# A fused bucketed attention and expert layer: row products split into gate products and plain transposes, with the head and tail order rewritten

## The chip, the core and the metric

The kernel runs on one core of a Trainium2 chip. Times are device microseconds (us) of one execution. The profile is one further execution of the same program, with every instruction of every engine recorded. Engines are called as in the profile: PE (TensorE matmul), PEld (its weight load, which runs beside PE), DVE (VectorE), ACT (ScalarE), POOL (GpSimd), SP (the engine that issues most transfers).

## The reference

```python
def attention(q, k, v, proj):                    # 4 batches, 8 heads, 768 rows, 64 columns
    mask = bucket(q @ proj > 0) == bucket(k @ proj > 0)     # 6 bits each
    scores = where(mask, q @ k.T / 8, -1e9)
    return softmax(scores) @ v

def experts(x, w_gate, w1, w2):                  # x: 3072 rows of 512
    logits = x @ w_gate                          # 8 experts
    e = argmax(logits); gate = softmax(logits)[e]
    return gate * (relu(x @ w1[e]) @ w2[e])      # 512 -> 1024 -> 512
```

## The kernel before

**Attention.** The 32 heads are taken as 16 pairs of heads (`g`), each pair as two halves of 384 query rows (`u`, 32 in all). A pair has 12 score units (`S0` to `S11`, one tile of 128 queries against 768 keys each, four products in fp32r). DVE takes the maximum (`R`), ACT the exponential (`X`), PE transposes the result in blocks of 128 (`T`), ACT or DVE copies them out (`E`), PE multiplies with V (`V`, 24 instructions for one half), ACT copies the result to the tile `ot` (`O`), which has the 128 columns of the two heads as partitions and 384 rows.

**Back to rows.** The step `K` (`tok`) turns `ot` into rows: for each of three blocks of 128 rows one f32 product with `ot` as the loaded weights and the 144 columns of `wgt` as the moving side. The 144 columns are 8 gate columns of the one head, an identity of 128, and 8 gate columns of the other head, so that one product gives rows and logit parts. `L` (`tok_ev`, DVE) scales them by 1/sum into `xr`. An f32 product is two MATMUL instructions, each with a weight load of its own; a plain transpose is one.

**Experts.** `route` (steps `r`) finds each row's expert and its slot, `scatter` (steps `c`) has POOL write three blocks of rows to `sorted_rows` in DRAM. Phase 0 are the first 256 rows of the largest expert, phase 1 the rest of its 512 rows; `rows(1)` loads these after the last scatter. `mm1` (steps `m`) and `mm2` are the two products; `xt` transposes the next phase's rows. Within `mm2(0, 1, mid)` the function `mid` calls `xts(1, (0, 1))`, the first two of the four transposing steps of phase 1. Weights are split into two fp32r parts by POOL (steps `v`, 1.9 us each).

**What sets the order.** Every engine works its instructions in program order. The order of the attention is written out by hand in three lists of step names: `HEAD` for pair 0, `PLAN` for pairs 1 to 14, `LAST` for pair 15, where a trailing `-` means the pair before. A letter at the end of a step (`A`, `V`, `P`, `a`, `v`) says which engine takes it. In `HEAD` the steps `k q j l p` cut the inputs into fp32r parts, `y` are the bucket products, `b` their signs, `f0` and `f1` the two parts of score unit 0, `i2` two idle products. Before `HEAD`, `warmth` issues `WARM` idle products on PE.

Of the kernel before, what the change touches and what calls it, by code (L numbers as in the profile page):

```python
# [7 lines left out]
F32 = mybir.dt.float32  # L8
# [7 lines left out]
B, H, S, D = 4, 8, 768, 64  # L16
# [25 lines left out]
FILL = 512  # L42
NONE = 1 << 20
TMAX = 24
WARM = 8


def tiles_of(n):
# [5 lines left out]
def lsh_attention_moe(ctx, tc, qk, qk2, v, proj, wg, w1, w2, out):  # L54
# [97 lines left out]
    def late_consts():  # L152
        tri = const.tile([128, 128], BF16, name="tri")
        nc.vector.tensor_scalar(tri, jp, 0.0, None, op0=OP.is_gt)
        C.update(tri=tri, ones=ones)
        C["desc"] = iota_f([128, E], [[-1, E]], "desc", base=E)
        C["base0"] = iota_f([128, E], [[ROW, E]], "base0")
        C["base"] = const.tile([128, E], F32, name="base")
        nc.vector.tensor_copy(C["base"], C["base0"])
        C["tokid"] = iota([128, B * NT], [[128, B * NT]], "tokid", cm=1)  # L160
        C["spacer"] = const.tile([1, 1], F32, name="spacer")
        nc.gpsimd.tensor_copy(wgt[:, :, E:PW - E], ident[:, None, :].to_broadcast([128, NP, 128]))
        empty_rows()

        C["oh"] = const.tile([128, 2 * 3 + 1, E], BF16, name="oh")
        nc.vector.memset(C["oh"], 0.0)
        C["ohs"] = const.tile([128, 2, 4, E], BF16, name="ohs")
        nc.vector.memset(C["ohs"], 0.0)
        C["ex"] = const.tile([128, 2 * 3, E + 1], F32, name="ex")
        nc.vector.memset(C["ex"], 1e-9)  # L170
# [198 lines left out]
    def tok(u):  # L369

        p = ps.tile([128, 512], F32, name="t", bufs=2)
        ot = OT.pop(u)
        x = p[:, :3 * PW].rearrange("p (t w) -> p t w", t=3)
        for t in range(3):
            nc.tensor.matmul(x[:, t], ot[:, t * 128:(t + 1) * 128], wgt[:, u // 2 % NP], start=True, stop=True)  # L375
        return x

    def tok_ev(u, p):
# [362 lines left out]
    def yout(n, j, mid=None):  # L741
        r, o, c = PH[n]
        if j >= len(tiles_of(c)):
            return
        i, pw = tiles_of(c)[j]
        if n + 1 == len(PH) and j + 1 == len(tiles_of(c)):
            youts(n, j, i, pw)
            return
        p = ps.tile([128, 512], F32, name="s", bufs=3)
        if by_token(n):  # L750
            k = 0
            for f in range(8):
                w = CH[4 * r + 2 + f // 4]
                for a, b in ((0, 0), (1, 0), (0, 1)):
                    nc.tensor.matmul(p[:pw], HH[n][b][:, f, i:i + pw], w[:, a, f % 4],  # L755
                                     start=(k == 0), stop=(k == 23))
                    k += 1
                    if k == 12 and mid:
                        mid()
        else:  # L760

            yw = max(pw, min(128, CAPS[1] - i))
            for m in range(4):
                nc.tensor.transpose(p[:yw, m * 128:(m + 1) * 128], YT[n][:, m, i:i + yw], ident)  # L764
        y = (P2["p"] if n else moe).tile([128, DM], F32, name="y" if n else "ye", bufs=3 if n else 2)
        nc.vector.tensor_scalar(y[:pw], p[:pw], GT[n][:pw, j:j + 1], None, op0=OP.mult)  # L766
        nc.gpsimd.memset(C["spacer"], 0.0)
        st = nc.gpsimd.indirect_dma_start(out=out, out_offset=bass.IndirectOffsetOnAxis(ap=IX[n][:pw, j:j + 1], axis=0),  # L768
                                          in_=y[:pw], in_offset=None, bounds_check=N - 1, oob_is_err=False)
        for q in outs:  # L770
            tc.declare_no_dep(st.ins, q.ins, reason="rows of other tokens")
        outs.append(st)
# [29 lines left out]
    load_x(2)  # L802
    load_x(3)
    load_v(0)
    for s in range(2):
        nc.sync.dma_start(wgt[:, :, s * (PW - E):s * (PW - E) + E], wg[:, :, s * E:(s + 1) * E])
    NC = NU // 2
    routes, parts, pick = {}, list(range(16)), pick_first()

    def weights(n):  # L810
# [8 lines left out]
    SPLITS = ((0, 0), (0, 1), (0, 2), (0, 3), (1, 0), (1, 1), (1, 2), (1, 3), (0, 4), (0, 5), (1, 4), (1, 5))  # L819

    HEAD = """
        k01V y01 k00A j01V j00P p00A y00 i2 q00V l00V b03 p01P b02 b00 q01P f0 b01 q10P k11A f1 p10A j11P y11 R0
        k10A S1 q11A j10P b13 G R1 X0 l10P y10 S2 b10 b12 s01 S3 X1 p11P R2 l01P H S4 b11 X2 R3 T00 E00a T01 w S5
        E01a R4 X3 T02 s00 E02a R5 T10 l11P X4 s10 S6 X5 E10v T11 S7 R6 E11a T12 s13 E12a R7 T20 X6 S8 s12 T21 E20v
        X7 S9 s03 s11 E21v T22 R8 s14 T30 E22a s02 S10 E30a R9 T31 z0 V0 E31a s15 X8 X9 M0 z1 s04 T32 O0 R10 S11 s05
        E32a T40 X10 R11 K0
    """.split()

    PLAN = """
# [4 lines left out]
    """.split()  # L834

    LAST = """
        S0 E40a- L0- X11- T41- R0 T42- E41a- S1 E42a- T50- R1 S2 T51- X0 E50a- X1 S3 R2 E51a- T52- S4 E52v- R3 T00
        T01 X2 E00a S5 E01a R4 T02 X3 V1- X4 E02v R5 X5 x0 M0 O1- M1- T10 T11 g0 E10v S6 E11a h0 T20 T12 R6 E20a S7
        E12a K1- R7 T21 S8 L1- X6 X7 S9 E21v T22 R8 E22a T30 x2 V0 R9 X8 E30a X9 g2 h2 T31 O0 S10 E31a T32 R10 T40
        E32a S11 K0 X10 v1 m0 R11 L0 E40a T41 m1 v1 r0 X11 E41a T42 v1 m2 u0 E42a d0 u1 d1 T50 r0 m3 T51 u2 r0 d2 v1  # L840
        E50a M1 v1 u3 T52 E52v E51a d3 m4 v1 u4 V1 d4 v1 v1 r0 O1 r0 K1 r0 r0 m5 L1 r1 u5 c0 r1 m6 r1 d5 u6 r1 m7 r1
        r1 r1 d6 c1 u7 d7
    """.split()

    DEAL = {"R5": 1, "E12a": 2, "T20": 1, "R8": 1, "M0": 1}
# [49 lines left out]
    def step(g, w):  # L895
# [29 lines left out]
        elif op == "K":  # L925
            TK[2 * n + int(x)] = tok(2 * n + int(x))
        elif op == "L":
            tok_ev(2 * n + int(x), TK.pop(2 * n + int(x)))
        elif op == "G" and n + 1 < NG:
            lsh_mm(n + 1)  # L930
        elif op == "H" and n + 1 < NG:
            lsh_ev(n + 1)
            if n:
                lsh_bits(n + 1)
        elif op in "kjqlp":
            cut(op, int(x[0]), int(x[1]), x[2])
        elif op == "y":
            lsh_first(int(x[0]), int(x[1]))
        elif op == "b":
            bits_first(int(x[0]), int(x[1]))  # L940
        elif op == "f":
            if x == "0":
                before(0)
            score(0, (x == "1",))
        elif op == "i":
            warmth(ps.tile([128, 2, 512], F32, name="s", bufs=3)[:, 0], int(x))
        elif op == "s":
            split(2 + int(x[0]), int(x[1]))
        elif op == "z":
            mask(2 + int(x))  # L950
        elif op == "w":
            lsh_bits(1)
        elif op in "xgh":
            xt_first(op, int(x))
        elif op == "m":
            mm1(0, int(x))
        elif op in "ud":
            relu(op, int(x))
        elif op == "r":
            go(last[int(x)], 1)  # L960
# [141 lines left out]
```

## Time and profile before

| | |
|---|---|
| Median of three runs | 774.7 us (771.43, 774.7, 774.88) |
| The profiled execution's own time | 777.09 us |
| its span, first to last instruction | 775.3 us |
| PE busy, share of the span | 763.9 us, 99% |
| PEld, ACT, POOL, DVE busy | 81%, 62%, 61%, 55% |

The span is what the instructions take; 1.8 us of the profiled execution lie around it. A busy PE is not PE at its peak, since the ends of its pipelined instructions are modelled; the pace is better read from one start to the next.

### The profile page before, as it was taken

The page shows a single profiled execution, that of the slowest core. Times are in us where ns is not written, and L with a number is a line of the kernel's source. Part 1 is how long each engine was busy: PE and PEld are TensorE (multiplying, and loading weights), DVE is VectorE, ACT ScalarE, POOL GpSimd, SP SyncE. Part 2 cuts the span into 40 slices and gives each one's busy share as a digit, 9 for nine tenths or more (in the row PEclk, how much of TensorE's full clock was granted, in tenths as well). Part 3 has the DMA queues.
Part 4 walks back from the last instruction along what each step waited for, and adds up shares of the span by engine and source line. Part 5 has one row for each costly group of instructions (what it writes and reads, how often), then busy time and mean ns, then how long its engine had stood idle before and what let it go on. Part 6 is the DMA issues. An engine that isn't in the chain of part 4 may idle for free.

```text
span 775.3 us, 13575 instructions
## 1 busy us (share of the span) xinstructions
PE 763.9 (99%) x4819; PEld 631.0 (81%) x4819; DVE 426.6 (55%) x1017; ACT 478.3 (62%) x936; POOL 474.8 (61%) x584
## 2 busy tenths in 40 slices
PE   9999999999999999999999998999999999999996
PEld 4777878777787777778778786989999999989895
DVE  6766766867676776667688653222454522232221
ACT  5888878878887887888788731443434444434320
POOL 7675465578635767754777482784665656668532
PEclk9999999999999999999999999999999999999998
DMA  7488844245314344530533225663445466545200
GB/s 268 163 254 271 296 160 154 70 149 185 128 62 163 123 137 160 163 103 21 163 128 120 82 95 169 233 225 105 167 140 178 144 111 197 169 149 185 101 10 36
DMA packets 48229, 115.12 MB, mean 148 GB/s; under 512 B 8851, under 2 KB 12691, under 8 KB 48160
## 3 DMA queue, kind: packets, MB, share of 16 engines
q1 hardware_dynamic: 41328, 97.88, 38.7%
q0 software_dynamic: 6688, 16.35, 6.2%
q8 instruction: 38, 0.62, 0.3%
q14 instruction: 31, 0.25, 0.1%
q10 hardware_dynamic: 144, 0.02, 0.0%
HBM read 88.39 MB, written 26.33 MB: 148 GB/s over the span
## 4 chain that ended last, share of the span: by engine, by line
PE 90%; issue 4%; POOL 2%; DVE 1%; DMA 1%; ACT 1%; SPq 0%; POOLq 0%; another core or an unknown queue 0%; DVEq 0%; ACTq 0%
PE t L320 17%; PE s L698 16%; PE t L356 16%; PE s L735 10%; PE s L288 9%; PE s L286 9%; PE s L755 6%; PE t L375 3%; PE t L244 2%; PE t L660 2%; PE s L764 1%; POOL w L626 1%; POOL sorted_rows L449 1%; PE t L222 1%; DVE m L296 1%
## 5 line engine op out<-in xcount | busy, mean ns | idle before, releaser
L296 DVE TENSOR_REDUCE m<-s 128x1 f32<-128x768 f32 x192 | 182.8, 952 | 97.8 <-PE s L288 84.6
L306 ACT ACTIVATE e<-s,m 128x768 f32<-128x768 f32 x192 | 190.8, 994 | 19.6 <-DVE m L298 12.7
L626 POOL TENSOR_TENSOR w<-raw,w 128x512 fp32r<-128x512 f32 x112 | 142.2, 1292 | 44.6 <-ACT w L625 43.3
L346 ACT ACTIVATE pt<-t 128x512 f32<-128x512 f32 (+1 forms) x254 | 143.7, 592 | 32.8 <-PE t L320 30.1
L320 PE MATMUL t<-ident,e 128*128 128x128 f32 x1152 | 161.7, 276 | 0.8 <-ACT e L306 0.3
L320 PEld LDWEIGHTS t<-ident,e 128*128 128x128 f32 x1152 | 133.4, 141 | 34.8 <-issue 13.2
L356 PE MATMUL t<-pt,vt 128*64 128x384 f32 x768 | 130.9, 490 | 0.0
L698 PE MATMUL s<-xh,w 128*128 128x456 f32 (+6 forms) x672 | 126.9, 346 | 0.0
L698 PEld LDWEIGHTS s<-xh,w 128*128 128x128 f32 x672 | 119.2, 188 | 3.0
L356 PEld LDWEIGHTS t<-pt,vt 128*64 128x64 f32 x768 | 52.3, 137 | 62.2 <-issue 59.9
L714 DVE SCALAR_TENSOR_TENSOR hh<-s,hh 128x256 fp32r<-128x256 f32 (+7 forms) x64 | 35.5, 555 | 90.8 <-ACT hh L712 89.3
L712 ACT ACTIVATE hh<-s 128x256 fp32r<-128x256 f32 (+7 forms) x64 | 31.4, 490 | 78.0 <-PE s L698 78.0
L735 PE MATMUL s<-hh,w 128*128 128x456 f32 (+3 forms) x384 | 78.7, 358 | 0.0
L735 PEld LDWEIGHTS s<-hh,w 128*128 128x128 f32 x384 | 69.9, 188 | 2.3
L768 POOL DMA_INDIRECT out_dram<-y,ix x26 | 25.9, 996 | 68.5 <-DVE y L766 30.7
L625 ACT ACTIVATE w<-raw 128x512 fp32r<-128x512 f32 x112 | 66.3, 623 | 0.0
L755 PE MATMUL s<-w,hh 128*128 128x512 f32 (+1 forms) x240 | 58.9, 398 | 0.0
L286 PE MATMUL s<-qk 80*128 80x384 f32 x192 | 57.9, 385 | 0.0
L286 PE MATMUL s<-w 80*128 80x384 f32 x192 | 56.9, 377 | 0.0
L254 POOL TENSOR_SCALAR bits<-bits,wsg 64x384 f32<-64x384 f32 x15 | 18.6, 1243 | 56.7 <-ACT bits L227 56.7
L288 PE MATMUL s<-qk 128*128 128x384 f32 x192 | 51.9, 352 | 0.0
L755 PEld LDWEIGHTS s<-w,hh 128*128 128x128 f32 (+1 forms) x240 | 43.9, 187 | 9.5
(199 smaller groups left out, 1025.6 us busy)
## 6 DMA issues: line engine op xcount, KB each, us to landing
raw<-in_w_dram SPq DMA_DIRECT2D x64, 512.0 KB, 3.7
xd<-in_qk_dram SPq DMA_DIRECT2D x17, 768.0 KB, 4.3
xhe<-in_qk_dram SPq DMA_DIRECT2D x15, 768.0 KB, 7.9
w<-in_qk_dram SPq DMA_DIRECT2D x14, 768.0 KB, 4.4
sorted_rows<-xr SPq DMA_DIRECT2D x8, 1156.0 KB, 13.9
xg<-sorted_rows SPq DMA_DIRECT2D x25, 289.0 KB, 5.0
vt<-in_v_dram SPq DMA_DIRECT2D x16, 384.0 KB, 3.6
masks<-bits SPq DMA_DIRECT2D x15, 192.0 KB, 1.9
```

Of the source, the lines that this page charges most:

```text
L286: nc.tensor.matmul(p[:, a, :HALF], k[0:80, 2, c], k[0:80, 3, n], start=i >= 4, stop=i < 4)
L288: nc.tensor.matmul(p[:, a, :HALF], k[:, 0, c], k[:, 1, n], start=i < 4, stop=i >= 4)
L296: nc.vector.tensor_reduce(m[:, 0:1], p[:, :, :HALF], axis=AX.XY, op=OP.max)
L306: nc.scalar.activation(e, p[:, :, :HALF], AF.Exp, bias=m[:, 2:3], scale=m[:, 1:2], accum_out=SM[g, hf][:, t, s:s + 1])
L320: nc.tensor.transpose(p[:, x * 128:(x + 1) * 128], e[w][:, kt // 3, (kt % 3) * 128:(kt % 3) * 128 + 128], ident)
L346: nc.scalar.activation(o, x, AF.Copy)
L356: nc.tensor.matmul(p[s * 64:(s + 1) * 64, :HALF], VT[g][:, kt, s, :], PT[u][:, s, kt, :], start=(kt == 0), stop=(kt == NT - 1))
L625: nc.scalar.activation(w[:, 0, a], r, AF.Copy)
L626: nc.gpsimd.tensor_tensor(w[:, 1, a], r, w[:, 0, a], op=OP.subtract)
L698: nc.tensor.matmul(p[:, :c], w[:, a, d, fs], x[:, b, d, :c], start=(k == 0), stop=(k == 11))
L735: nc.tensor.matmul(p[:, :c], w[:, a, f % 4, ms], h[b][:, f, :c], start=(k == 0), stop=(k == 23))
L755: nc.tensor.matmul(p[:pw], HH[n][b][:, f, i:i + pw], w[:, a, f % 4], start=(k == 0), stop=(k == 23))
```

## The change

The step `K` is taken apart: three f32 products of 16 columns (the gate columns alone), written to columns 0 to 7 and 136 to 143 of each block of 144, and then three plain transposes of the same blocks of `ot` into columns 8 to 135. For the second and third block the slice begins 128 columns lower, for the addressing alone. `wgt` no longer holds the identity, so a POOL copy goes, and one DMA brings it where two did. `WARM` goes from 8 to 10, and `i2` leaves `HEAD`. `HEAD` and `LAST` are written anew. In `mm2(0, 1, mid)` the call of `mid` moves from after 12 of the 24 products to after 20; for other phases it stays at 12.

```diff
-WARM = 8
+WARM = 10
...
-    wgt = const.tile([128, NP, PW], F32, name="wgt")
+    wgt = const.tile([128, NP, 2 * E], F32, name="wgt")
...
-        nc.gpsimd.tensor_copy(wgt[:, :, E:PW - E], ident[:, None, :].to_broadcast([128, NP, 128]))
...
         for t in range(3):
-            nc.tensor.matmul(x[:, t], ot[:, t * 128:(t + 1) * 128], wgt[:, u // 2 % NP], start=True, stop=True)
+            a = 0 if t == 0 else PW - E - E
+            o = p[:, t * PW - a:t * PW - a + 2 * (PW - E)].rearrange("p (s w) -> p s w", s=2)[:, :, a:a + E]
+            nc.tensor.matmul(o, ot[:, t * 128:(t + 1) * 128], wgt[:, u // 2 % NP], start=True, stop=True)
+        for t in range(3):
+            nc.tensor.transpose(x[:, t, E:PW - E], ot[:, t * 128:(t + 1) * 128], ident)
...
-                    if k == 12 and mid:
+                    if k == (12 if n else 20) and mid:
...
-    for s in range(2):
-        nc.sync.dma_start(wgt[:, :, s * (PW - E):s * (PW - E) + E], wg[:, :, s * E:(s + 1) * E])
+    nc.sync.dma_start(wgt, wg)
...
-        k01V y01 k00A j01V j00P p00A y00 i2 q00V l00V b03 p01P b02 b00 q01P f0 b01 q10P k11A f1 p10A j11P y11 R0
...
+        q01P k00A k01V y01 j01V q00A j00V y00 p01P l00V p00A b00 f0 b03 b02 q10P k11A p10A y11 b01 k10A f1 R0 j11P
...
-        E50a M1 v1 u3 T52 E52v E51a d3 m4 v1 u4 V1 d4 v1 v1 r0 O1 r0 K1 r0 r0 m5 L1 r1 u5 c0 r1 m6 r1 d5 u6 r1 m7 r1
...
+        E51a d2 E52a m3 u3 r0 r0 M1 V1 d3 v1 r0 r0 O1 c0 K1- K1 m4 L1- L1 v1 r1 m5 r1 r1 u4 d4 v1 r1 r1 m6 r1 u5 r1
```

What the lists do to the engines is seen from the order of instructions. On PE, at the end of the last pair, from the last V product (L356) over the slot products of `route` (L421, L424), `K1` (L375) and the hidden products `mm1` (L698, twelve for each step `m`) to `mm2`. Before:

```order
L356 MATMUL t<-pt,vt 64x384 x12
L421 LDWEIGHTS tri
L421 MATMUL t<-ohs,tri 128x32
L424 LDWEIGHTS ones
L424 MATMUL t<-ohs,ones 128x24
L424 LDWEIGHTS ones
L424 MATMUL t<-ohs,ones 128x16
L424 LDWEIGHTS ones
L424 MATMUL t<-ohs,ones 128x8
L375 MATMUL t<-wgt,ot 128x144 x3
L698 MATMUL s<-xhe,w_5411 128x256 x24
```

The same place in the change, where line numbers are three or four higher:

```order
L355 MATMUL t<-pt,vt 64x384 x12
L376 MATMUL t<-wgt,ot 128x2x8 x3
L378 MATMUL t<-ident,ot 128x128 x3
L376 MATMUL t<-wgt,ot 128x2x8 x3
L378 MATMUL t<-ident,ot 128x128 x3
L701 MATMUL s<-xhe,w_5471 128x256 x24
```

The slot products moved ahead of the V product, `K1` of the pair before (`K1-`) came between V and `K1`, and twelve hidden products (`m4`) that stood before V now stand behind `K1`: 48 of them follow it, where 36 did.

On PE a little further on, the second products of phase 0 (`mm2`, L755) and the transposes of phase 1's rows (L660). Before:

```order
L698 MATMUL s<-xhe,w_5411 128x256 x12
L755 MATMUL s<-w_5552,qk 128x512 x12
L755 MATMUL s<-w_5651,qk 128x512 x12
L755 MATMUL s<-w_5552,qk 128x512 x12
L660 MATMUL t<-ident,xd 128x128 x4
L755 MATMUL s<-w_5651,qk 128x512 x12
L660 MATMUL t<-ident,xd 128x128 x4
```

In the change (L701, L758 and L663 are the same lines):

```order
L701 MATMUL s<-xhe,w_5471 128x256 x24
L758 MATMUL s<-w_5630,qk 128x512 x12
L758 MATMUL s<-w_5721,qk 128x512 x12
L758 MATMUL s<-w_5630,qk 128x512 x12
L758 MATMUL s<-w_5721,qk 128x512 x8
L663 MATMUL t<-ident,xd 128x128 x4
L758 MATMUL s<-w_5721,qk 128x512 x4
L663 MATMUL t<-ident,xd 128x128 x4
```

The first four transposes stand behind 44 products of `mm2`, before behind 36, and only four products now lie between the two groups of transposes.

On POOL, the scatter of the last batch's first half (`c0`) and second half (`c1`), in the change:

```order
L449 COPY xr<-tokid_i 128x3
L451 MEMSET spacer 1x1
L452 DMA sorted_rows<-xr,slot 25600x578
L451 MEMSET spacer 1x1
L452 DMA sorted_rows<-xr,slot 25600x578
L451 MEMSET spacer 1x1
L452 DMA sorted_rows<-xr,slot 25600x578
L625 CAST w_5721<-raw 128x512
L626 TENSOR_TENSOR w_5721<-raw,w_5721 128x512
L625 CAST w_5721<-raw 128x512
L626 TENSOR_TENSOR w_5721<-raw,w_5721 128x512
L449 COPY xr<-tokid_i 128x3
```

Before, the two scatters followed each other directly behind the eighth weight part; now `c0` stands two weight parts earlier and these two parts lie between `c0` and `c1`.

## Rows read from the trace of the kernel before

**Rows 1.** From the page: span, busy time of each engine, and the shares of the engines in the chain that ended last.

```profile
span 775.3 us, 13575 instructions
PE 763.9 (99%) x4819; PEld 631.0 (81%) x4819; DVE 426.6 (55%) x1017; ACT 478.3 (62%) x936; POOL 474.8 (61%) x584
PE 90%; issue 4%; POOL 2%; DVE 1%; DMA 1%; ACT 1%; SPq 0%; POOLq 0%; another core or an unknown queue 0%; DVEq 0%; ACTq 0%
```

**Rows 2.** Busy time by engine in the middle of the attention, 50 to 440 us.

```profile
50.00:440.00 390.00, 389.56 (x2714) 298.45 (x2714) 277.47 (x680) 319.54 (x618) 243.08 (x326) 1.00 0.45 149
```

**Rows 3.** All groups by line: the products and the weight loads of `K` and of transposes, and the weight load of `mm1` of phase 0 (count, then busy us and mean ns of one).

```profile
L375 PE MATMUL t<-wgt,ot 128*128 128x144 f32 x192 | 28.9, 286 | 0.4 <-ACT ot L361 0.4
L320 PE MATMUL t<-ident,e 128*128 128x128 f32 x1152 | 161.7, 276 | 0.8 <-ACT e L306 0.3
L375 PEld LDWEIGHTS t<-wgt,ot 128*128 128x128 f32 x192 | 26.3, 190 | 0.5 <-ACT ot L361 0.5
L320 PEld LDWEIGHTS t<-ident,e 128*128 128x128 f32 x1152 | 133.4, 141 | 34.8 <-issue 13.2 <-ACT pt L346 9.5 <-DVE rf L409 1.8
L698 PEld LDWEIGHTS s<-xhe,w 128*128 128x128 f32 x192 | 23.6, 191 | 0.1
```

**Rows 4.** PE in order of time at three places: eight transposes and what follows, one `K` without a wait (its six weight loads first), and the last `K` behind a wait (start, us from the group's first start to its last end, count; in brackets the idle time before).

```profile
131.50 1.04 PE L320 MATMUL t<-ident,e 128*128 128x128 f32 x8
...
135.62 0.85 PEld L375 LDWEIGHTS t<-wgt,ot 128*128 128x128 f32 x6
135.79 0.90 PE L375 MATMUL t<-wgt,ot 128*128 128x144 f32 x6
136.62 4.09 PE L356 MATMUL t<-pt,vt 128*64 128x384 f32 x24
...
459.07 1.00 PE L375 MATMUL t<-wgt,ot 128*128 128x144 f32 x6 [0.40 <-ACT ot L361]
459.81 3.12 PE L698 MATMUL s<-xhe,w 128*128 128x256 f32 x24
```

**Rows 5.** PE in order of time from the last V product's end to the second products of phase 0, and on to the transposes of phase 1; the last two lines are groups of the stretch from 464 to 473 us (busy us and mean ns of one).

```profile
458.41 0.19 PE L421 MATMUL t<-ohs,tri 128*128 128x32 bf16 x1
...
463.06 1.68 PE L698 MATMUL s<-xhe,w 128*128 128x256 f32 x12
464.57 8.57 PE L755 MATMUL s<-w,qk 128*128 128x512 f32 x36
...
474.16 0.30 PE L660 MATMUL t<-ident,xd 128*128 128x128 f32 x1 [1.02 <-DMA xd<-sorted_rows]
476.41 0.55 PE L660 MATMUL t<-ident,xd 128*128 128x128 f32 x3 [1.95 <-DMA xd<-sorted_rows]
476.71 4.60 PE L755 MATMUL s<-w,qk 128*128 128x512 f32 x12
481.15 0.60 PE L660 MATMUL t<-ident,xd 128*128 128x128 f32 x4
...
L755 PE MATMUL s<-w,qk 128*128 128x512 f32 x36 | 8.6, 396 | 0.0
L698 PE MATMUL s<-xhe,w 128*128 128x256 f32 x7 | 1.0, 283 | 0.0
```

**Rows 6.** Stretches around that wait: length, busy us of PE, PEld, DVE, ACT, POOL (instructions), granted clock as a share of full speed, share of the DMA engines, GB/s.

```profile
473.00:476.50 3.50, 0.53 (x3) 0.23 (x3) 0.04 (x1) 0.00 (x0) 0.00 (x0) 1.00 0.62 200
476.50:477.70 1.20, 1.20 (x7) 1.05 (x8) 0.64 (x4) 0.66 (x2) 0.00 (x0) 1.00 0.00 0
477.70:481.10 3.40, 3.40 (x9) 2.54 (x8) 0.31 (x1) 0.00 (x0) 0.00 (x0) 0.50 0.85 296
```

**Rows 7.** In order of time, what the rows of phase 1 wait for: DVE's last `tok_ev` and the end of its `route`, POOL's first scatters of `c0` and `c1`, the last scatter, SP's load of the rows.

```profile
459.52 0.18 DVE L439 RECIPROCAL xr<-rf 128x3 f32<-128x3 f32 x1
460.11 0.61 DVE L385 TENSOR_TENSOR xr<-t,r 128x432 f32<-128x432 f32 x1 [0.41 <-PE t L375]
460.52 1.08 POOL L449 DMA_INDIRECT sorted_rows<-xr,slot  x1 [1.89 <-issue]
464.09 0.18 DVE L439 RECIPROCAL xr<-rf 128x3 f32<-128x3 f32 x1
465.05 0.98 POOL L449 DMA_INDIRECT sorted_rows<-xr,slot  x1 [0.65 <-POOL spacer L448]
467.61 0.96 POOL L449 DMA_INDIRECT sorted_rows<-xr,slot  x1 [0.22 <-issue]
471.19 0.90 SPq L640 DMA_DIRECT2D xd<-sorted_rows  x2
```

**Rows 8.** PE in order of time over the head.

```profile
1.07 3.60 PE L105 MATMUL t<-ones 128*128 128x512 bf16 x8 [1.07 <-DVE warm L97]
4.60 2.02 PE L222 MATMUL t<-xd,pj 64*32 64x384 f32 x8
6.55 1.03 PE L105 MATMUL s<-ones 128*128 128x512 bf16 x2
...
8.80 1.49 PE L222 MATMUL t<-xd,pj 64*32 64x384 f32 x4
...
11.79 1.51 PE L244 MATMUL t<-xhe,pj 128*32 128x384 f32 x8
...
18.66 1.84 PE L320 MATMUL t<-ident,e 128*128 128x128 f32 x8
```

**Rows 9.** In order of time: the second head's inputs reach the cutting engine (ACT, waiting for its DMA).

```profile
8.35 0.94 ACT L214 ACTIVATE qk<-xd 128x384 fp32r<-128x384 f32 x2 [0.99 <-DMA xd<-in_qk_dram]
```

More of the change, by code (lines that the diff above doesn't have):

```diff
@@ L821, in lsh_attention_moe @@
     HEAD = """
-        k01V y01 k00A j01V j00P p00A y00 i2 q00V l00V b03 p01P b02 b00 q01P f0 b01 q10P k11A f1 p10A j11P y11 R0
[L823 to L826, printed above, removed]
+        q01P k00A k01V y01 j01V q00A j00V y00 p01P l00V p00A b00 f0 b03 b02 q10P k11A p10A y11 b01 k10A f1 R0 j11P
+        p11A S1 G j10P b13 y10 R1 S2 X0 l01P b12 l10P b10 R2 X1 S3 H S4 b11 R3 X2 T00 T01 E00a R4 S5 R5 w q11P s11
+        l11P E01a T02 X3 E02a X4 T10 S6 s10 E10v T11 s13 S7 s12 R6 X5 E11a T12 T20 E12a R7 X6 z1 s01 S8 T21 E20v X7
+        S9 T22 E21v s05 R8 E22a T30 E30a S10 R9 T31 s00 s02 X8 R10 s03 V0 z0 X9 E31v M0 O0 T32 s04 s15 X10 S11 s14
+        E32v T40 R11 K0
     """.split()
@@ L836, in lsh_attention_moe @@
     LAST = """
[L837 to L840, printed above, removed]
-        E50a M1 v1 u3 T52 E52v E51a d3 m4 v1 u4 V1 d4 v1 v1 r0 O1 r0 K1 r0 r0 m5 L1 r1 u5 c0 r1 m6 r1 d5 u6 r1 m7 r1
-        r1 r1 d6 c1 u7 d7
+        S0 E40a- X11- L0- R0 S1 T41- T42- S2 R1 E41a- X0 T50- E42v- E50a- X1 R2 S3 T51- T52- S4 E51a- E52v- R3 T00
+        T01 X2 S5 E00a T02 E01a V1- X3 R4 X4 E02v R5 X5 T10 O1- E10a S6 T11 E11a R6 T12 S7 E12a R7 T20 S8 X6 T21 S9
+        E20a X7 T22 E21v x0 R8 E22a T30 V0 g0 X8 R9 E30v X9 x2 O0 h0 T31 M0 g2 E31a S10 S11 T32 h2 E32a R10 T40 m0
+        K0 E40a v1 v1 R11 L0 T41 X10 X11 E41a m1 r0 u0 v1 M1- T50 u1 T42 E50v d0 r0 m2 E42a r0 v1 T51 T52 u2 d1 v1
+        E51a d2 E52a m3 u3 r0 r0 M1 V1 d3 v1 r0 r0 O1 c0 K1- K1 m4 L1- L1 v1 r1 m5 r1 r1 u4 d4 v1 r1 r1 m6 r1 u5 r1
+        m7 c1 d5 u6 d6 u7 d7
     """.split()
@@ L945, in step @@
         elif op == "i":
-            warmth(ps.tile([128, 2, 512], F32, name="s", bufs=3)[:, 0], int(x))
+            warmth(SC.setdefault(int(x[0]), ps.tile([128, 2, 512], F32, name="s", bufs=3))[:, 0], int(x[1]))
         elif op == "s":
```

## The prediction

> **What bounds the kernel now.** I read the page's busy times first, then the busy time by engine of single stretches, then PE in order of time. PE is busy 763.9 of 775.3 us and makes 90% of the chain that ended last; the other engines are far below [rows 1]. In the middle of the attention PE is busy 389.56 of 390 us, while ACT has 70 us to spare there and DVE over 110 [rows 2]. So each microsecond that PE's own instructions gain or lose there is one of the whole time, and nothing that DVE, ACT or POOL do for longer shows, as long as PE doesn't wait. PE's losses that are not its own work stand in two places: in the head, where it runs at half pace [rows 8], and behind the last pair, where it waits for the rows of phase 1 [rows 5].
>
> "Busy" hides how PE spends its time, so I price by starts. A group of n equal instructions that takes a time t from the first start to the last end, with d for one, has its starts (t - d)/(n - 1) apart.
>
> **Step K, 32 times.** Before, six MATMUL instructions of 144 columns: (0.90 - 0.286)/5 = 0.123 us from start to start [rows 3, 4]. Each has a load of 128 weight columns of its own. The loads run one product ahead: the first starts at 135.62 for a product at 135.79, the last at 135.62 + 0.85 - 0.19 = 136.28 for a product at 135.79 + 0.90 - 0.286 = 136.40 [rows 3, 4]. What such a load costs when nothing hides it is seen at the last K, behind a wait: the six take 1.00 where they take 0.90 otherwise, so 0.10 us [rows 4]. A load for a transpose is cheaper: behind the wait for the second tile, three transposes take 0.55 us; less 0.276 for the last that is 0.274 for two gaps, of which one is the usual (1.04 - 0.276)/7 = 0.109, the other 0.165, so the load costs 0.06 [rows 3 to 5].
>
> After, the six products have 16 columns instead of 144. By columns one would take 0.12 x 16/144 = 0.013 us, far less than its load. No row here shows so short an f32 product. Its pace lies between 0.013 (the load hidden by something) and 0.123 (nothing gained, as now). I take the load: it can only start when the product before it starts, and it takes 0.10, so 0.105 from start to start. From the first start to the last: five gaps of 0.105, one of 0.06 to the first transpose, two of 0.109, in all 0.80 us, where five gaps of 0.123 made 0.615. The last instruction is a transpose (0.109) where it was a product (0.123), which gives 0.01 back. That is +0.18 us for one K, and 32 x 0.18 = **+5.8 us**, all on PE's path [rows 2]. With both bounds: at 0.013 the sum is 0.065 + 0.06 + 0.218 = 0.34, so -0.27 for one and -8.8 us; at 0.123, and with a full 0.109 before the first transpose, +0.31 and +10.0 us.
>
> The rows show a load of about 0.10 us that must lie between two short products. The Trainium skill, TensorE: Matmul & The Clock Gate, section Back-to-back issue gap, gives a product of up to 64 columns about 60 cycles, 25 ns; its section LDWEIGHTS (loading the stationary operand) gives a load its columns at 1.2 GHz whatever the product, which is 107 ns for 128. The second speaks against this change, and the 0.10 us of the row agrees with it; by the first alone K would come to 0.40 us, -0.22 for one and an estimated -7 us in all. What the first would do here is the first rival below.
>
> **The end of the last pair.** Three things move, all towards the same wait. Before, `mm2` starts at 464.57, 36 products at (8.57 - 0.396)/35 = 0.234 us end at 472.98; the four transposes take 0.44, so without a wait `mm2` would go on at 473.42. It goes on at 476.71: **3.3 us** lost [rows 5]. From 477.70 the granted clock is 0.50, the lower level (1.2 GHz), for 3.4 us with PE busy throughout, after a stretch of 3.5 us in which PE was busy 0.53 [rows 6]: **1.7 us** more. And `K1` waits 0.40 us for `ot` and shows its load, 0.10: **0.5 us** [rows 4].
>
> After: I count from the end T of `K1`, before at 459.81. The chain to the rows (`tok_ev` from T + 0.3, the end of `route` at T + 4.5, the scatters until T + 8.8, the load issued at T + 11.4, the tiles used at T + 14.35 and T + 16.6) hangs on `K1` and is not shortened [rows 4, 5, 7]. PE gets more to do before it needs them. From `K1` to `mm2` it took 464.57 - 459.81 = 4.76 us with 36 hidden products; 12 more at (1.68 - 0.283)/11 = 0.127 add 1.5 [rows 5]. Then 44 products of `mm2` instead of 36 take 10.3. So PE comes to the transposes at T + 16.6: the first tile is there, the second just arrives; I put 0.1 us. With no idle stretch I expect no fall of the clock either. `K1-` now runs while ACT copies `ot` for `K1`, so that wait goes as well. On the other side, only four products (0.93 us) lie between the two groups of transposes, too short for copying the first two `t` tiles out and for the last of `xh`: 0.3 us. Sum: -3.3 + 0.1 - 1.7 - 0.5 + 0.3 = **-5.1 us**. The bounds: -5.5, if nothing is waited for, and 0, if the rows come as much later as PE does.
>
> What could make them late is POOL. `c1` stands behind `c0` and, newly, behind two weight parts of 1.9 us. In the trace a first scatter starts 0.8 us after `route` has ended (459.70 to 460.52, 464.27 to 465.05), then one every 1.3 [rows 7]. In the change the slot products stand ahead of V, some 4 us earlier against V's end, and POOL has two weight parts less to do before `c0`. `route`'s end, 1.2 us after V before, comes 2.9 ahead of V's end, the first scatter 2.1 ahead; `c0` ends 1.5 us after V, the two parts at 5.3, and `c1` can't start before T + 4.4, which is 6.2 after V with a `K1-` of 0.9 and a `K1` in between. That leaves 0.9 us.
>
> **The head.** All of PE's work up to 20 us runs at half pace: idle products of 512 columns every (3.60 - 0.63)/7 = 0.42 us, eight transposes in 1.84 us that later take 1.04 [rows 4, 8]. Ten idle products in all before and after; two go from 6.55 to the front. The first ones then end near 5.3, the bucket products of head 0 near 6.7, `f0` at 7.4; then PE waits for head 1, whose inputs come at 8.35, do `y11`, `f1` and `S1`, and reach `G` near 11.7. Before it did so at 11.79 [rows 8, 9]. So **0**, between -1 and +1 for the order of cuts and signs. The POOL copy and the second DMA of `wgt` that go lie beside this and cost nobody anything. If the clock rose earlier it would be more; that is a rival.
>
> **Sum.** +5.8 - 5.1 + 0 = +0.7 us. The profiled execution took 777.09, so 777.8; it stands 2.4 above the median of the runs, and I take the same step from the median: 775.4 us. From no change a measurement of this kernel can tell about 0.5%, 3.9 us, so this is no change.
>
> **The rivals.**
> *Short products hide their loads* (pace 0.013 to 0.03): K gains 7 to 9 us, and with the end's 5.1 the time is about 761. For it: the change's sense, and that loads of 0.19 us apiece are overlapped at a pace of 0.127 in `mm1` [rows 3, 5]. Against it: there the products themselves are longer than the 0.10 that a load costs. Chance 8%.
> *K costs more* (the other side): a product of any width keeps the pace of 0.123 and the first transpose waits its turn: +10.0 - 5.1 = 779.6, slower by 0.6%. It decides from a K of about +0.28 us on. For it: no row shows an f32 product faster than 0.123. Chance 15%.
> *The clock rises early.* Ten unbroken idle products bring PE to 2.4 GHz near 5 us. Then the 11.8 us of work from 8.4 to 20.2 halve at most, less what POOL's cuts hold up: some 4 us, so 771. Against it: eight of them did not do it, and PE would then stand idle from about 6.4 to 8.35, and an idle stretch is what went before the clock's fall at 477.7 [rows 6, 8]. Chance 12%.
> *The rows of phase 1 are as late as before*, since `c1` is held by the weight parts, or the tiles land later: 3 to 5 us back, 779. Chance 5%.
>
> **How the numbers follow.** The forecast (K by its load, the wait gone, the head as it was) has 60%. By itself it lies between 772 and 779, from 0.105 +/- 0.01 for the pace (1.6 us) and 2 us that the end may keep. The range of 769 to 780.5 takes in the slow cases and the early clock and leaves out the hidden loads and tails. Faster by over 0.5% (below 770.8): the 8%, half of the 12%, a tail of 3%, so 0.17. Slower by over 0.5% (above 778.6): most of the 15%, the 5% and a tail, so 0.20. Within: 0.63.
>
> **What would show it.** Right: six products in K about 0.105 apart, K 0.19 longer from its first start to the next line's; a wait for phase 1's rows under 0.5 us; no stretch of 0.50 after 470 us; `mm2`'s first product at T + 6.3; eight transposes near 18.7 us still in 1.84. Wrong: products closer than 0.09 or wider than 0.115; `c1`'s first scatter later than T + 5.5; PE waiting in the last pair at a place where it did not before, above all for `t` tiles.

## The result, and the profile after

The change made the kernel slower: 779.4 us against 774.7, medians of five runs each, ratio 1.0081 [1.0055, 1.0106]. The ratio, with its 95% interval, is not the quotient of these two medians (1.0060); the five runs of the kernel before lie between 771.4 and 777.4. The forecast was "no change", 775.4; the time lies in the range but on its slow side.

The profiled execution of the changed kernel took 778.83 us, 1.7 more than that of before. From the page, the span and the busy times:

```profile
span 777.1 us, 13769 instructions
PE 764.8 (98%) x4915; PEld 636.1 (82%) x4915; DVE 429.5 (55%) x1020; ACT 479.2 (62%) x934; POOL 474.0 (61%) x582
```

PE is still busy nearly throughout [rows 1], so each microsecond that it gains or loses must be found on PE. The 1.7 us are the sum of three differences of either sign. They are separated by where the V products stand. The first of the 32 halves' V products and the thirtieth's, PE in order of time, in the change:

```profile
26.66 0.54 PE L355 MATMUL t<-pt,vt 128*64 128x384 f32 x2
428.60 0.87 PE L355 MATMUL t<-pt,vt 128*64 128x384 f32 x4
```

and the same two before:

```profile
29.68 0.54 PE L356 MATMUL t<-pt,vt 128*64 128x384 f32 x2
425.77 0.54 PE L356 MATMUL t<-pt,vt 128*64 128x384 f32 x2
```

**The head** ends 3.0 us earlier. PE works there at the upper level early on: four bucket products that took 1.49 us before [rows 8] take 0.83.

```profile
7.26 0.83 PE L221 MATMUL t<-xd,pj 64*32 64x384 f32 x4 [0.30 <-ACT qk L226]
```

**The 29 halves between** take 401.94 us instead of 396.09: 5.85 more, 0.20 for each half, so 32 x 0.20 = 6.4 for the kernel. That is `K`. **The end** gets what is left: 1.7 + 3.0 - 6.4 = -1.7 us, where -5.1 was forecast.

**`K` in the change.** All groups by line (count, then busy us and mean ns of one), and one `K` in order of time, its matrix loads first:

```profile
L376 PEld LDWEIGHTS t<-wgt,ot 128*128 128x128 f32 x192 | 24.8, 191 | 0.6 <-issue 0.6
L376 PE MATMUL t<-wgt,ot 128*128 128x16 f32 x192 | 23.7, 249 | 0.0
```

```profile
447.89 0.76 PEld L376 LDWEIGHTS t<-wgt,ot 128*128 128x128 f32 x6
...
448.00 0.74 PE L376 MATMUL t<-wgt,ot 128*128 128x16 f32 x6
448.59 0.52 PE L378 MATMUL t<-ident,ot 128*128 128x128 f32 x3
448.95 0.60 PE L319 MATMUL t<-ident,e 128*128 128x128 f32 x4
```

The six loads start (0.76 - 0.191)/5 = 0.114 us apart, where those of before with 144 columns behind each started (0.85 - 0.19)/5 = 0.13 apart [rows 4]. A product with a ninth of the columns is hardly faster, and the three transposes come on top: from the first of the six to the next line it takes 0.95 us. That the load alone sets this pace is tested below (k_wide). The Trainium skill, TensorE: Matmul & The Clock Gate, section LDWEIGHTS (loading the stationary operand), makes a load of 128 columns 107 ns; the 114 ns of the rows come near it.

**The end of the last pair in the change,** PE in order of time:

```profile
460.68 0.74 PE L376 MATMUL t<-wgt,ot 128*128 128x16 f32 x6
461.27 0.53 PE L378 MATMUL t<-ident,ot 128*128 128x128 f32 x3
461.55 3.12 PE L701 MATMUL s<-xhe,w 128*128 128x256 f32 x24
466.43 0.19 PE L424 MATMUL t<-ohs,tri 128*128 128x32 bf16 x1 [1.76 <-DVE ohs L419]
...
466.55 4.31 PE L701 MATMUL s<-xhe,w 128*128 128x256 f32 x24
470.66 10.79 PE L758 MATMUL s<-w,qk 128*128 128x512 f32 x44
481.29 0.60 PE L663 MATMUL t<-ident,xd 128*128 128x128 f32 x4
```

The transposes of phase 1's rows (L663) wait for nothing any more, the waits on `K1` are gone too. But the slot products (L424) now wait 1.76 us for DVE, where the slot products of before waited for nothing (no bracket behind the one in [rows 5]), and the 24 hidden products behind them take 4.31 us, which took 3.12 ahead of them. The stretches around show why (columns as in [rows 6]):

```profile
463.00:466.40 3.40, 1.67 (x14) 1.47 (x13) 3.17 (x8) 0.82 (x3) 3.21 (x5) 1.00 0.14 56
...
468.00:471.40 3.40, 3.40 (x16) 3.30 (x16) 0.56 (x3) 0.77 (x2) 2.44 (x5) 0.50 0.27 99
```

PE idles from 464.7 to 466.4, and from 468.0 on the granted clock is at the lower level for 3.4 us, as it was before behind the wait for the rows [rows 6]. The same loss stands at another place. What DVE did in that time, and what POOL did (start, us):

```profile
463.02 0.18 DVE L412 TENSOR_REDUCE rf<-rl 128x3 f32<-128x24 f32 x1
463.24 1.00 DVE L413 TENSOR_TENSOR rl<-rl,rf 128x24 f32<-128x24 f32 x1
464.27 0.52 DVE L414 TENSOR_SCALAR rl<-rl 128x24 f32<-128x24 f32 x1
464.82 0.18 DVE L415 TENSOR_TENSOR rl<-rl,desc 128x24 f32<-128x24 f32 x1
465.25 0.92 DVE L418 TENSOR_TENSOR rl<-desc,rf 128x24 f32<-128x24 f32 x1
466.20 0.18 DVE L419 TENSOR_SCALAR ohs<-rl 128x24 bf16<-128x24 f32 x1
```

```profile
462.90 1.29 POOL L626 TENSOR_TENSOR w<-raw,w 128x512 fp32r<-128x512 f32 x1
464.14 0.61 POOL L625 CAST w<-raw 128x512 fp32r<-128x512 f32 x1
464.83 1.29 POOL L626 TENSOR_TENSOR w<-raw,w 128x512 fp32r<-128x512 f32 x1
...
468.53 1.00 POOL L452 DMA_INDIRECT sorted_rows<-xr,slot  x1 [2.24 <-DVE qk L717]
```

Three of DVE's operations on 24 columns take 1.00, 0.52 and 0.92 us where others of the same size take 0.18. Each of the three ends within 0.05 us of a POOL instruction: 464.24 and 464.19, 464.79 and 464.75, 466.17 and 466.12. The POOL instructions belong to the two weight parts that the new `LAST` put between `c0` and `c1`. The last row is the first scatter of `c1`, 6.98 us after the end of `K1` at 461.55; in after_parts below it starts 5.17 us after it. Together the three cost the chain (1.00 + 0.52 + 0.92) - 3 x 0.18 = 1.9 us, just about the wait. That POOL is the cause is tested below (parts_ahead).

### The profile page after: what moved, and what is told of

Read it like the earlier page. It is cut to its first block, busy times and chain, and to the rows that moved or that the text cites. A ratio compares the mean times of both kernels' runs of the same rounds, so it can differ in the third digit from the quotient of the medians.

```text
span 777.1 us, 13769 instructions
## 1 busy us (share of the span) xinstructions
PE 764.8 (98%) x4915; PEld 636.1 (82%) x4915; DVE 429.5 (55%) x1020; ACT 479.2 (62%) x934; POOL 474.0 (61%) x582
## 4 chain that ended last, share of the span: by engine, by line
PE 92%; issue 3%; POOL 1%; ACT 1%; DVE 1%; DMA 0%; POOLq 0%; SPq 0%; another core or an unknown queue 0%
PE t L319 17%; PE s L701 17%; PE t L355 17%; PE s L738 10%; PE s L285 9%; PE s L287 9%; PE s L758 7%; PE t L376 2%; PE t L663 2%; PE t L243 2%; PE t L378 1%; PE s L767 1%; POOL w L629 1%; ACT e L305 1%; DMA xd<-in_qk_dram 0%
## 5 line engine op out<-in xcount | busy, mean ns | idle before, releaser
L345 ACT ACTIVATE pt<-t 128x512 f32<-128x512 f32 (+1 forms) x251 | 141.6, 591 | 32.7 <-PE t L319 29.8
L701 PE MATMUL s<-xh,w 128*128 128x456 f32 (+6 forms) x672 | 126.9, 346 | 0.0
L701 PEld LDWEIGHTS s<-xh,w 128*128 128x128 f32 x672 | 119.2, 188 | 3.0
L758 PE MATMUL s<-w,hh 128*128 128x512 f32 (+1 forms) x240 | 58.9, 398 | 0.0
L758 PEld LDWEIGHTS s<-w,hh 128*128 128x128 f32 (+1 forms) x240 | 43.9, 187 | 9.5
L669 DVE TENSOR_TENSOR xh<-t,xh 128x456 fp32r<-128x456 f32 (+6 forms) x28 | 16.0, 575 | 64.2 <-ACT xh L668 63.9
```

The costliest lines, as they stand in the source:

```text
L345: nc.scalar.activation(o, x, AF.Copy)
L701: nc.tensor.matmul(p[:, :c], w[:, a, d, fs], x[:, b, d, :c], start=(k == 0), stop=(k == 11))
```

## The experiments

The ratios are to the kernel before, which ran beside each experiment (4 to 12 executions of each, 23 or 29 of the kernel before, whose medians there are 771.4 to 772.1 us). "First V" is the start of the first V product in the profiled execution, "rest" the span less that: it leaves the head out.

| | median us | ratio [95%] | first V | rest |
|---|---|---|---|---|
| before, the profile of the rows ahead | 774.7 | 1 | 29.7 | 745.6 |
| after | 779.4 | 1.0081 [1.0055, 1.0106] | 26.7 | 750.4 |
| before_again | 772.4 | 1.0002 [0.9988, 1.0016] | 30.0 | 742.3 |
| k_only | 779.9 | 1.0096 [1.0064, 1.0128] | 26.0 | 750.0 |
| k_wide | 781.0 | 1.0111 [1.0087, 1.0136] | 29.6 | 752.4 |
| no_k | 774.9 | 1.0020 [0.9997, 1.0042] | 28.7 | 744.3 |
| last_only | 772.8 | 1.0001 [0.9976, 1.0025] | 25.9 | 744.2 |
| mid_only | 769.7 | 0.9971 [0.9953, 0.9988] | 25.7 | 742.3 |
| parts_ahead | 768.2 | 0.9953 [0.9935, 0.9971] | 27.4 | 740.3 |
| after_parts | 777.7 | 1.0069 [1.0046, 1.0092] | 28.8 | 746.9 |
| head_only | 773.8 | 1.0017 [1.0002, 1.0032] | 29.8 | 742.7 |
| head_hold | 774.7 | 1.0034 [1.0018, 1.0051] | 26.0 | 743.9 |
| warm10 | 770.9 | 0.9990 [0.9978, 1.0001] | 26.5 | 742.6 |
| list12 | 774.4 | 1.0026 [1.0011, 1.0041] | 29.6 | 743.2 |
| best1 | 771.1 | 0.9976 [0.9961, 0.9991] | 28.8 | 740.6 |
| best2 | 768.1 | 0.9956 [0.9940, 0.9971] | 26.1 | 740.5 |

### The parts one by one

**k_only**: the kernel before with the new `K` and its smaller `wgt`, nothing else of the diff.

> Only the step K is taken apart (three products of 16 columns, three plain transposes); lists, WARM and the place of mid are those of before. Theory: a short product is paced by its weight load; in the trace of the change the products follow each other every 0.112 us and the first transpose behind them at 0.112, the second at 0.142, so one K is 0.20 us longer and 32 of them cost +6.4 us: about 0.8% slower than before, and the V products of the middle pairs fall behind by 0.20 us for each half. Rival: part of the loss of the change is the lists', then K alone costs under 3 us.

**last_only**: the kernel before with the new `LAST` and `mid` after 20 products.

> Only the list LAST and the place of mid (after 20 of 24 products) are changed; K, HEAD and WARM are those of before. Theory: the wait for the rows of phase 1 (3.3 us) goes, but the slot product of the last route now waits about 1.8 us for DVE, whose small operations are held up by the two weight parts that POOL works between the two scatters, and the clock falls behind that wait instead of behind the other: 1.5 to 2 us faster than before in like runs. The prediction's view: no new wait, no fall of the clock, 5 us faster.

**head_only**: the kernel before with the new `HEAD` and `WARM` at 10.

> Only HEAD and WARM = 10 are changed. Theory: ten unbroken idle products bring the clock to its upper level near 4 to 5 us in most runs, and the first V product stands near 26.7 us instead of 29.7: runs lie 2 to 3 us under those runs of before in which the clock rises near 20 us, and the spread of runs is smaller than the 6 us of before. Prediction's view: no change of the head, first V product at 29.7 +/- 1.

**no_k**: the change with the old `K`.

> The change with K as before (three f32 products of 144 columns): HEAD, WARM, LAST and mid are the new ones. If K is the whole loss, 779.4 - 6.4 = 773 us, 1.5 to 2 us under the median of before (0.2% faster). If the lists themselves cost time, it stays above 775.

`K` alone makes the kernel slower by as much as the whole change, and without it nothing slower can be told: `K` is the loss. The new end by itself gives nothing (1.0001): its slot products wait for DVE as in the whole change, 2.26 us, and the clock falls behind that wait, as expected, but of the 1.5 to 2 us that it was to gain, 1.4 show against the first profile of before (rest 744.2 against 745.6) and none in the ratio. The new head loses a little (1.0017), where 2 to 3 us less were expected; in its profile the clock was up at 5.8 us, fell at 9.3, and the first V stood at 29.8, not 26.7. no_k came to 774.9, between the two cases of its expectation. The ratios of k_only, last_only and head_only add up to 1.0114, somewhat over the 1.0081 of the whole change.

In last_only, a DVE operation, the POOL instruction at work meanwhile, and the slot product:

```profile
456.23 1.29 DVE L411 TENSOR_SCALAR rl<-rl 128x24 f32<-128x24 f32 x1
...
456.20 1.28 POOL L623 TENSOR_TENSOR w<-raw,w 128x512 fp32r<-128x512 f32 x1
...
459.69 0.19 PE L421 MATMUL t<-ohs,tri 128*128 128x32 bf16 x1 [2.26 <-DVE ohs L416]
```

The longest stretch here falls on an operation with one tile as input, which ends 0.04 us behind POOL's.

### Does the number of columns matter in `K`?

**k_wide**: the new `K` with products of 96 columns, zeros between the gate columns, instead of 16.

```diff
-    wgt = const.tile([128, NP, 2 * E], F32, name="wgt")
+    wgt = const.tile([128, NP, 96], F32, name="wgt")
+    nc.gpsimd.memset(wgt, 0.0)
...
-            o = p[:, t * PW - a:t * PW - a + 2 * (PW - E)].rearrange("p (s w) -> p s w", s=2)[:, :, a:a + E]
+            o = x[:, t].rearrange("p (s w) -> p s w", s=3)[:, 0:3:2]
```

> K taken apart as in the change, lists of before, but the three products have 96 columns instead of 16 (the gate columns at both ends of zeros; the plain transposes then write over the zeros). By columns a product takes 0.12 x 96/144 = 0.08 us instead of 0.013. Theory (the weight load paces short products): still 0.112 us from start to start and the same time as with 16 columns, about 779 us. Rival (each product pays its columns on top of a fixed price): 0.067 us more for each of six, 0.4 for one K, 13 us in all, about 792 us.

PE in order of time, a `K` and the first and thirtieth V product:

```profile
29.58 0.87 PE L356 MATMUL t<-pt,vt 128*64 128x384 f32 x4
431.86 1.51 PE L356 MATMUL t<-pt,vt 128*64 128x384 f32 x8
450.55 0.80 PE L376 MATMUL t<-wgt,ot 128*128 128x96 f32 x6
451.19 0.49 PE L378 MATMUL t<-ident,ot 128*128 128x128 f32 x3
```

402.28 us from V to V, 6.19 more than before, against 5.85 with 16 columns in the change and 5.57 in k_only, which has the same lists as k_wide. Six times as many columns cost 0.01 to 0.02 us per half, where the rival has 0.4: from the first of the six to the first transpose it is 0.64 us here and 0.59 with 16 columns. So the loads set the pace between 16 and 96 columns. The median, 781.0, is near the 779 of the theory and far from the 792 of the rival.

### What holds up the slot products?

**parts_ahead**: as last_only, with the two weight parts ahead of `c0` instead of between `c0` and `c1`.

```diff
-        E51a d2 E52a m3 u3 r0 r0 M1 V1 d3 v1 r0 r0 O1 c0 K1- K1 m4 L1- L1 v1 r1 m5 r1 r1 u4 d4 v1 r1 r1 m6 r1 u5 r1
+        E51a d2 E52a m3 u3 r0 r0 M1 V1 d3 v1 r0 r0 O1 v1 v1 c0 K1- K1 m4 L1- L1 r1 m5 r1 r1 u4 d4 r1 r1 m6 r1 u5 r1
```

> The kernel with only LAST and mid changed, but with POOL's last two weight parts ahead of the first scatter instead of between the two. Theory (POOL's weight parts hold up DVE's small two-input operations): the last route takes about 1.7 us less from its first reduction to the slots' one-hot, the slot product on PE waits under 0.3 us instead of 1.8, nothing falls idle for long behind the last V product and the clock stays up to the end: 2 to 3.5 us faster than with the parts between the scatters. Rival (the operations are slow by themselves, or the wait is for the rescaling of the pair before): the wait of 1.8 us stays.

DVE's operations and PE in order of time:

```profile
457.55 0.18 DVE L410 TENSOR_TENSOR rl<-rl,rf 128x24 f32<-128x24 f32 x1
457.77 0.18 DVE L411 TENSOR_SCALAR rl<-rl 128x24 f32<-128x24 f32 x1
458.42 0.18 DVE L415 TENSOR_TENSOR rl<-desc,rf 128x24 f32<-128x24 f32 x1
```

```profile
458.87 0.19 PE L421 MATMUL t<-ohs,tri 128*128 128x32 bf16 x1
...
458.99 3.12 PE L698 MATMUL s<-xhe,w 128*128 128x256 f32 x24
461.94 10.43 PE L755 MATMUL s<-w,qk 128*128 128x512 f32 x44
472.21 0.60 PE L660 MATMUL t<-ident,xd 128*128 128x128 f32 x4
```

The same three operations take 0.18 us each, the slot products wait for nothing, 24 hidden products take 3.12 us behind them, and the rows of phase 1 are waited for neither. With the same work on every engine, in another order on POOL alone, the rest is 3.9 us shorter than in last_only, the ratio 0.9953 against 1.0001, with intervals apart, and the kernel is faster than before by 0.5%. So the weight parts beside the DVE chain are the cause of the wait.

**after_parts**: the whole change with the same two parts moved in the same way.

> The change whole, with one thing moved: the two weight parts that stand between c0 and c1 go ahead of c0. Theory (in the change DVE's small operations of the last route are stretched while POOL works these parts, so the slot products wait 1.76 us and the clock falls behind the wait): the operations take 0.18 us each, no wait at the slot products, no stretch of 0.50 after 460 us, about 3.5 us less than the change: 776, ratio 1.004 to the kernel before; the 6.4 us of the K split stay. Rival (the loss of the change sits in K alone and the end gives nothing more): 779.4, ratio 1.009.

In the profile the theory holds: the slot products don't wait, the clock does not fall, and the rest is 750.4 - 746.9 = 3.5 us shorter than that of the change. The whole time doesn't show it: 1.0069 against 1.0081, intervals that overlap, and not the 1.004 expected. In the two profiles the heads differ by 2.1 us the other way, at least part of the reason; the ratios of the parts (k_only, parts_ahead, head_only) add up to 1.0066. So the gain is shown from the first V on, and not in the median.

**mid_only**: the kernel before with `mid` after 20 products in phase 0 and nothing else.

> Only the place of mid is changed, after 20 of the 24 products of the second block instead of after 12. Eight more products, 1.9 us, stand ahead of the transposes of phase 1. Theory: where the rows come 1.8 to 3.3 us late it takes back up to 1.8 us; less 0.3 us, since only four products lie between the two groups of transposes. So 0.5 to 1.5 us faster, 0.1 to 0.2%. Rival: the rows' landing is what PE waits for at the next place (the second group) and nothing is gained.

PE in order of time, the transposes of the second tile of phase 1's rows:

```profile
472.41 0.55 PE L660 MATMUL t<-ident,xd 128*128 128x128 f32 x3 [1.01 <-DMA xd<-sorted_rows]
```

Its rest is 742.3, that of before_again below, but its rows came later. PE could use the second tile 16.5 us after T (the end of `K1`, here 455.88), about as late as in the first profile of before (16.6) and later than in before_again (14.7). With rows that late the old place lost 3.0 us of waiting and then the clock [rows 5, 6]; here the wait is 1.0 us and the clock stays up. So `mid` takes back part of the wait where the rows come late, as the theory has it, and its ratio of 0.9971 is clear of 1. The head need not be the reason: the profiled execution has the earliest first V of all and took 769.9 us, while five of the other eleven took 768.3 to 768.8, less than any of the 29 of before (769.85 at the least). How much of the gain is the end's in those is not shown.

### Was the profiled execution of before like its others?

**before_again**: the kernel before, profiled again.

> The kernel before, unchanged, for a second profile. Theory (the profiled execution of before was not like its median: the clock rose late, at 20.3, and fell once behind the wait for phase 1's rows): the clock rises before 6 us, the first V product starts near 26 instead of 29.7, the wait for the rows is 1.8 to 3.3 us, and the span is near 770 to 772. Rival (that profile was the usual one): the clock rises near 20 and falls at 477, span 775.

PE in order of time from the second products of phase 0 to the transposes of phase 1's rows:

```profile
465.02 8.57 PE L755 MATMUL s<-w,qk 128*128 128x512 f32 x36
474.22 0.30 PE L660 MATMUL t<-ident,xd 128*128 128x128 f32 x1 [0.63 <-DMA xd<-sorted_rows]
474.98 0.55 PE L660 MATMUL t<-ident,xd 128*128 128x128 f32 x3 [0.46 <-DMA xd<-sorted_rows]
475.28 3.05 PE L755 MATMUL s<-w,qk 128*128 128x512 f32 x12
```

The waits are 1.1 us, not the 3.0 of [rows 5], the clock does not fall behind them (12 products in 3.05 us, 4.60 in [rows 5]), and the rest is 3.3 us shorter. The profiles of head_only and warm10, which have the same end, agree (742.7 and 742.6). Over the eight profiles with the old end the waits for these rows are 1.1 to 2.2 us in six, without a fall of the clock behind them, and 3.0 us in two, with it: the first profile of before, and k_wide's. The head, though, was as in the first profile: a clock at the lower level until about 20 us, first V at 30.0. So one half of the expectation held and the other did not.

### The head

**head_hold**: head_only with two idle products behind `y00` and six ahead of `y10`, to fill PE's idle stretches.

> Only HEAD and WARM changed, with eight more idle products: two ahead of score unit 0 and six ahead of the bucket products of head 1's other half, where PE stands idle in the new HEAD. Theory: the new HEAD loses the clock in these gaps once it is up; with the gaps filled the granted clock stays at its upper level from about 5 us on, the first V product stands near 26.3 us, and the time is 2 to 3 us under that of the new HEAD alone. Rival: the new order itself, not the clock, costs the time: then the first V product stays near 28 us or later.

**warm10**: the kernel before with `WARM` at 10, the old list with its `i2`.

> Only WARM from 8 to 10, with the old head list and its i2: twelve idle products instead of ten. Theory (the new list of the head, not the number of idle products at the front, costs the 1.3 us that the new head loses): the clock rises near 5 and stays up, first V product near 26, ratio 0.998 to 1.001. Rival (more idle products at the front only delay the head): first V product 0.4 to 0.8 later, ratio 1.001 to 1.002.

**list12**: the new list with `WARM` at 12, so as many idle products as warm10 has in all.

> The new list of the head with twelve idle products in front, two more than the change; old K, old end. Theory (the new list loses the clock, since PE stands idle for 1.8 us before the bucket products of the last cuts): the clock is up before 6 us and at 0.50 for some us between 9 and 20, first V product 27 to 30, ratio 1.001 to 1.003. Rival (twelve idle products, as in warm10, hold the clock whatever the list): no stretch of 0.50 in the head, first V product near 26.3, ratio 0.998 to 1.000.

PE in order of time at `y10`, and the stretch that follows (columns as in [rows 6]), of the change, of list12 and of warm10:

```profile
11.91 0.83 PE L221 MATMUL t<-xd,pj 64*32 64x384 f32 x4 [1.78 <-ACT qk L226]
...
14.00:17.40 3.40, 3.40 (x16) 3.30 (x15) 3.20 (x8) 1.68 (x3) 3.25 (x5) 0.51 0.21 87
```

```profile
13.27 1.33 PE L222 MATMUL t<-xd,pj 64*32 64x384 f32 x4 [1.77 <-ACT qk L227]
...
14.00:17.40 3.40, 3.40 (x11) 2.87 (x10) 1.78 (x4) 0.80 (x3) 2.49 (x3) 0.50 0.49 192
```

```profile
12.37 0.83 PE L222 MATMUL t<-xd,pj 64*32 64x384 f32 x4 [1.06 <-ACT qk L227]
...
14.00:17.40 3.40, 2.97 (x21) 2.73 (x20) 3.09 (x6) 1.77 (x4) 3.22 (x4) 1.00 0.54 174
```

With the new list PE stands 1.8 us before `y10` and then runs at the lower level; in warm10, with the old one, it stands 1.1 us and keeps the higher. Other profiles whose clock is up by then go the same way: it stays up behind 0.36 us (head_hold) and 0.75 to 1.02 (k_only, last_only, mid_only, best2), and falls behind 1.76 to 1.78 (after_parts, best1). But the old list can lose it too, as in parts_ahead, where it falls at 14.5 us behind this wait:

```profile
12.69 0.83 PE L222 MATMUL t<-xd,pj 64*32 64x384 f32 x4 [1.33 <-ACT qk L227]
```

And in head_only and no_k it falls ahead of `y10`, at 9.3 and 9.0 us, in no_k behind waits of 0.23 and 0.42 us alone.

With the same twelve idle products the two lists differ by 3.1 us at the first V and by 0.0036 of the ratio, 2.8 us, so at that number the list decides. The number at the front goes with the rise: in all nine profiles with ten or twelve idle products there the clock was up by 3.8 to 6.7 us; with eight it was up by 3.9 to 5.6 us in four and rose at about 20 us in three (before, before_again, k_wide). That the idle stretch at `y10` is the cause of the new list's loss is only argued: head_hold filled it, and its profiled execution did hold the clock (first V at 26.0), but its median was no better than head_only's. What happened in its other executions is open.

### Together

**best1**: the change with the old `K` and the weight parts ahead of `c0`.

> The change with the old K and with the two weight parts ahead of c0: new head, new end. Theory (new head +1.3, new end with the parts ahead -3.6): ratio 0.997, 769.8, with PE idle before y10 and y11 and the clock down for some us after it. Rival (the head costs nothing, its 1.0017 was scatter): ratio 0.9953, 768.4.

**best2**: parts_ahead with `WARM` at 10.

> Old K, old list of the head with WARM at 10, the new list of the last pair with both weight parts ahead of c0, mid after 20. Theory (the two gains add: the clock stays up in the head, and the end waits nowhere): first V product near 26.5, 740.3 from there to the end, span 766.8, ratio 0.993 to 0.995 to the kernel before. Rival (parts_ahead had a head with an early clock as it was, nothing is added): ratio 0.9953, 768.2.

best1 lies 0.0023 of the ratio, 1.8 us, above parts_ahead, from which it differs in the head alone: the new list's price a second time, though the intervals overlap. best2 gave what parts_ahead had given (0.9956, 0.9953). Its profile shows both gains, 26.1 to the first V and 740.5 for the rest, but the median shows no more than one. best2 and parts_ahead beat both kernels: by 0.0044 to 0.0047, some 3.5 us, the kernel before, and by 0.0125, some 9.6 us, the changed one. Of the first, `mid` alone gives 0.0029 (mid_only), and the intervals of mid_only and parts_ahead overlap, so what the new `LAST` adds to it is not shown.

## Why the prediction was wrong

**`K`, +5.8: right in mechanism, 10% short.** The load between short products is what costs. It is 0.114 us from load to load, not 0.105; since the first load had run ahead, the six products still start only (0.74 - 0.249)/5 = 0.098 apart on average. The mis-sized term is the step to the first transpose, 0.10 us (0.59 - 5 x 0.098) and not 0.06; the drift of the V products gives 6.4, inside the bounds. The rival of hidden loads is refuted; the rival "a product of any width keeps its pace" was near, since 16 and 96 columns go at one pace, but that pace is the load's 0.114 and not 0.123.

**The end, -5.1: the term that failed, by 3.4 us in the profile and more against the median.** It was to pay for `K`, and by itself it gave nothing: the ratio of last_only is 1.0001. The step that failed is "the chain to the rows hangs on `K1` and is not shortened". I checked what the two weight parts do to POOL's own queue (0.9 us to spare) and not what they do to DVE, which works the chain in that very time. It was lengthened: by 1.9 us of stretched operations, and `mm2` started at T + 9.1 instead of T + 6.3, with T the 461.55 of the rows above. "With no idle stretch I expect no fall of the clock" was right as a condition; the stretch had moved 15 us ahead, from the row transposes to the slot products. A rule of the Trainium skill speaks to it: SBUF — State Buffer, section Who interferes with whom, says that a DVE instruction with two SBUF inputs contends with a POOL instruction that reads SBUF, that the ports they share are an exclusive lock, and that the order of issue decides which of the two blocks. The rows agree: L413 and L418 ended with POOL's instruction, L415, which started 0.01 us ahead of POOL's next, took 0.18, and the reduction L412 took 0.18 with POOL at work. What it says of two inputs does not cover L414, with one, which took 0.52 (and 1.29 in last_only). Of the 1.9 us, 1.00 + 0.92 - 2 x 0.18 = 1.6 could have been estimated from this rule, the rows and the place of the parts.

**The base, 2.4 us: wrong.** I took the profiled execution's 777.09 for a median plus an offset that would stay, and credited the end with all that it lost there. It would not stay: before_again shows a wait of 1.4 us instead of 3.3 in the count of the prediction (465.02 + 36 x 0.234 + 0.44 = 473.88, and `mm2` goes on at 475.28), and no fall of the clock behind it. So a good part of the -3.3 and all of the -1.7 were no loss of the usual execution. Against that end the new one is no gain but a loss: 750.4 - 742.3 = 8.1 us, of which `K` makes 6.4 and the new wait with its clock the rest. From profile to profile the change cost 1.7 us where I had forecast 0.7, near it by luck, since the head's gain of 3.0 hid the end's miss of 3.4; from median to median it cost 4.7, and by the ratio some 6, as the 774.7 was high too: longer series of the kernel before have medians of 771.4 to 772.1.

**The head, 0: wrong in the profile.** It came 3.0 us earlier since the clock rose at about 4 us, the rival with 12%. What that rival has of ten unbroken idle products held in all nine profiles that have at least ten. The 3.0 us are luck of the two executions all the same: with eight the old list's clock rises that early in four profiles of seven (first V 25.7 to 26.0 in k_only, last_only and mid_only, 27.4 in parts_ahead), and the new list lost it again in six of its seven. By head_only's ratio, 1.0017 [1.0002, 1.0032], the new head is a loss of 1.3 us.

**The rival of late rows** ("`c1` is held by the weight parts") named the right two instructions for the wrong reason: they held up DVE and through it PE, and the rows then came before PE asked for them. Its sign, `c1`'s first scatter later than T + 5.5, did appear (it started at T + 7.0). So did the last sign of being wrong, PE waiting in the last pair where it did not before, though at the slot products and not for `t` tiles.

## What to carry to other kernels

Count weight loads, not columns: a product that loads its own 128 f32 columns has a floor of about 0.11 us here, so splitting one wide product into a narrow one and a transpose adds instructions and saves nothing. Before moving POOL work, look at what DVE does in the new place; small operations on a chain, with two inputs or one, can be held until POOL's instruction ends. And before crediting a removed stall in full, see whether a second profile of the same kernel has it.

## What the runs showed of the hardware

A two-input DVE operation of 0.18 us took up to 1.00 in the change while POOL worked on SBUF, and ended within 0.05 us of POOL's instruction; a one-input TENSOR_SCALAR took 0.52 in the same way, and 1.29 in last_only; a reduction took its 0.18. Six products of 16 and of 96 f32 columns with a load each take nearly the same, 0.59 and 0.64 us to the next instruction. And PE's granted clock fell to 0.50 behind single waits of 1.8 and 2.3 us at the slot products (the change, last_only) and of 1.3 to 1.8 us at `y10`, while it stayed at 1.00 behind 1.1 us of waiting, in two pieces in before_again and in one in warm10. In no_k it fell behind less, 0.23 and 0.42 us, so the length of a wait by itself does not tell.
